# Chunk-selected attention and a gated MLP on one core: eight-tile bounds, half-row scores, transposes by DMA, and a written order

## The chip, the core and the metric

The kernel runs on one core of a Trainium2 chip. The core has five engines with instruction queues of their own: TensorE (PE; matrix products and transpositions), VectorE (DVE), ScalarE (ACT), GpSimd (POOL) and SyncE (SP, which here only issues DMA transfers). They meet through semaphores alone: an engine takes its instructions in the order written, and a wait holds up all that is queued behind it. The metric is device time in microseconds (us). Before the change it is 266.71 us, the median of three runs (265.65 to 267.24). The profiled execution spans 262.9 us from its first to its last instruction.

## The reference

Two parts, over 4 batches of 768 rows.

Attention: 8 heads of 64 columns per batch, 32 heads in all. The keys of a head form 24 chunks of 32 rows. For each chunk the minimum and maximum of every key column are taken, and each query gets an upper bound of its score on each chunk:

```
ub = sum(max(q * k_min, q * k_max))          # q, k_min, k_max: 64 columns
ub = where(chunk of q >= chunk, ub, -1e9)
top_chunks = argsort(ub)[-6:]                # six chunks per query
mask = (chunk of key in top_chunks) & (row of q >= row of key)
attn = softmax(where(mask, q k^T / 8, -1e9)); x = attn v
```

The MLP, on x of shape 4 x 768 x 512:

```
u, v = split(gelu(x w_in))                   # 512 + 512 columns
v_n  = layernorm(v) * g_ln
out  = x + (u * (w_sg v_n + b_sg)) w_out     # w_sg mixes the 768 rows
```

## The kernel before

**Pairs and quads.** Two heads make a pair p (16 of them), two pairs a quad g (8). `loads` (L525) brings q, k and v as f32, 192 KB for each head, three buffers of each, never more than four transfers in flight (`WINDOW`). `kside` transposes k on PE in two halves of 384 rows (L540), takes the chunk minima and maxima on DVE (L546, into `W`; L559 turns the maxima into differences) and copies k^T to bf16 on ACT: L551 for the first four pairs, in two copies of 64 partitions to `KA` and `KB`, and L555 for the others, in one copy of 128 partitions, with a DMA moving the second head from `KA` to `KB` (L563) and another putting the chunk indicator `IND` beside it (L565). `qside` does the same with q (L575, L580), makes `rT` = max(q, 0) on DVE (L584) and casts q to bf16 on POOL (L587, L589, L592).

**Bounds and selection.** Since max(q kmin, q kmax) = q kmin + max(q, 0)(kmax - kmin), `select` computes the bounds of a quad as f32 products on PE (L613): two PSUM banks of 288 query rows each, and in a bank four tiles of 64x32 side by side, one for each head. Only rows from 192 on need it; earlier rows have at most six chunks. DVE transposes the bounds in 32x32 blocks (L621), finds the sixth largest (L629: 18 top-eight instructions), compares (L632) and transposes the result back: straight into `QA` and `QB` for the first two quads (L640), else into `Dt` (L644), from which DMA copies take it (L649). A chunk not selected is marked 1 there, and `IND` holds -480 on that chunk's keys, so that the product of the extended q and k is the score with the mask in it.

**Heads.** `head` multiplies q and k in blocks on or below the diagonal into two PSUM tiles of 1024 columns (L677), ACT takes the exponential (L682), POOL clears what lies above the diagonal (L686), PE multiplies with v, which has a column of ones (L696, L703), and DVE divides (L711, L713) into `XS`. When a pair is done, `xtrans` transposes its columns of x on PE (L723) and DVE copies them to `xT` (L727). w_sg is transposed in the same way, once (L735, L739).

**MLP of a batch.** When four pairs are done: `moe_h` computes v (L751, gelu L755, statistics L758 and L760, 1/sqrt on POOL L764, normalizing L767) and u (L777, gelu L782); `moe_g` mixes the rows (L794, on two PSUM banks), scales and adds the bias on DVE (L801, `vsT`), multiplies by u on DVE (L805), and multiplies by w_out (L814); DVE adds x (L820), and SP stores (L823). It runs among the attention of later pairs; the last batch's MLP stands alone at the end.

**The order.** `schedule` is a list planner: with costs and priorities it decides, when the kernel is built, each engine's order, and it gives PSUM slots and semaphores accordingly. The small PSUM tiles (four banks, PSG) are split by purpose. `fill` puts dummy products (L463) where PE would wait at the start, so that its clock stays up.

Of the kernel before, what the change touches and what calls it, by code (L numbers as in the profile page):

```python
# [13 lines left out]
LAT = {"pe": 0.15, "act": 0.20, "dve": 0.12, "pool": 0.15, "sp": 0.05}  # L14
TABLE_SWITCH = 1.3
WINDOW = 4


class PsumTile:


    def __init__(self, cls, slots=None):
        self.cls = cls
        self.slots = slots
        self.left = 0
        self.slot = None
        self.end = 0.0
        self.ops = []
# [6 lines left out]
class PsumClass:  # L35
    def __init__(self, aps):
        self.aps = aps
        self.owner = [None] * len(aps)

    def tile(self, slots=None):  # L40
        return PsumTile(self, slots)


class Op:
    __slots__ = ("eng", "fn", "cost", "prio", "deps", "dma", "ps", "alloc", "table", "burst",
                 "start", "end", "pos", "waits", "inc", "count", "idx", "lane", "bulk", "port")


class Program:
# [3 lines left out]

    def __init__(self):
        self.ops = []
        self.writer = {}
        self.readers = {}
        self.dma_sems = {}
        self.base = 0.0

    def op(self, eng, fn, cost, reads=(), writes=(), ps=(), alloc=None, dma=None, table=None,
           burst=None, prio=None, lane=0, bulk=False, port=False):
        o = Op()
        o.bulk = bulk
        o.port = port or (eng == "pool" and dma is None)
        o.lane = lane
        o.idx = len(self.ops)
        o.eng, o.fn, o.cost, o.dma, o.table, o.burst = eng, fn, cost, dma, table, burst
        o.prio = (self.base if prio is None else prio) + 1e-4 * o.idx
        deps = {}  # L70
        ps = tuple(ps) + ((alloc,) if alloc is not None else ())
        o.ps, o.alloc = ps, alloc
        for t in ps:
            t.left += 1
            for x in reversed(t.ops):
                if x.eng != eng:
                    deps.setdefault(x.idx, False)
                    break
            t.ops.append(o)
        for r in reads:  # L80
            w = self.writer.get(r)
            if w is not None:
                deps[w] = True
        for r in writes:
            w = self.writer.get(r)
            if w is not None:
                deps[w] = True
            for x in self.readers.get(r, ()):
                deps.setdefault(x, False)
        for r in reads:  # L90
            self.readers.setdefault(r, []).append(o.idx)
        for r in writes:
            self.writer[r] = o.idx
            self.readers[r] = []
        if dma is not None:
            last = self.dma_sems.setdefault(dma, [])
            if last:
                deps[last[-1]] = True
            last.append(o.idx)
        o.deps = deps  # L100
        self.ops.append(o)
        return o

    def schedule(self):
        ops = self.ops
        succ = [[] for _ in ops]
        ndep = [len(o.deps) for o in ops]
        alloc = {o.alloc: o for o in ops if o.alloc is not None}
        for o in ops:
            hold = set()  # L110
            for t in o.ps:
                a = alloc[t]
                if a is not o:
                    hold.update((d, a.idx) for d in o.deps if d < a.idx and d not in a.deps)
            for d, a in hold:
                if a not in succ[d]:
                    succ[d].append(a)
                    ndep[a] += 1
            for d in o.deps:
                succ[d].append(o.idx)  # L120
        ready = {e: [] for e in ENGINES}
        rt = [0.0] * len(ops)
        for o in ops:
            if ndep[o.idx] == 0:
                ready[o.eng].append(o.idx)
        free = {e: 0.0 for e in ENGINES}
        order = {e: [] for e in ENGINES}
        table = None
        burst_left = {}
        for o in ops:  # L130
            if o.burst is not None:
                burst_left[o.burst] = burst_left.get(o.burst, 0) + 1
        cur_burst = None
        pool_owner = {}

        def slot_for(t, now):
            best = None
            for i, own in enumerate(t.cls.owner):
                if t.slots is not None and i not in t.slots:
                    continue  # L140
                at = 0.0 if own is None else (own.end if own.left == 0 else None)
                if at is not None and (best is None or at < best[0]):
                    best = (at, i)
            return best

        n = 0
        dma_free = 0.0
        soft_free = 0.0
        flight = []
        held = {"pool": 0.0, "dve": 0.0}  # L150
        while n < len(ops):
            pick = None
            for e in ENGINES:
                cands = []
                for i in ready[e]:
                    o = ops[i]
                    t = max(rt[i], free[e])
                    if o.alloc is not None and o.alloc.slot is None:
                        s = slot_for(o.alloc, t)
                        if s is None:  # L160
                            continue
                        t = max(t, s[0] + 0.15)
                    if e == "act" and o.table is not None:
                        if cur_burst is not None and o.burst != cur_burst:
                            continue
                        if o.table != table:
                            t += 0.0
                    if o.port:
                        t = max(t, held["pool" if e == "dve" else "dve"])
                    if o.bulk and len(flight) >= WINDOW:  # L170
                        t = max(t, ops[flight[-WINDOW]].end)
                    cands.append((t, o.prio, i))
                if not cands:
                    continue
                tmin = min(c[0] for c in cands)
                best = min((c for c in cands if c[0] <= tmin + 0.02), key=lambda c: c[1])
                if pick is None or best[0] < pick[0]:
                    pick = (best[0], e, best[2])
            if pick is None:
                raise RuntimeError("no operation can be scheduled")  # L180
            t, e, i = pick
            o = ops[i]
            ready[e].remove(i)
            if o.alloc is not None and o.alloc.slot is None:
                at, s = slot_for(o.alloc, t)
                old = o.alloc.cls.owner[s]
                if old is not None:
                    for x in old.users:
                        o.deps.setdefault(x, False)
                o.alloc.slot = s  # L190
                o.alloc.cls.owner[s] = o.alloc
                o.alloc.users = []
            cost = o.cost
            if e == "act" and o.table is not None:
                if o.table != table:
                    cost += TABLE_SWITCH
                    table = o.table
                if o.burst is not None:
                    cur_burst = o.burst
                    burst_left[o.burst] -= 1  # L200
                    if burst_left[o.burst] == 0:
                        cur_burst = None
            o.start = t
            if o.port:
                held[e] = t + cost
            if o.bulk:
                if len(flight) >= WINDOW:
                    o.deps[flight[-WINDOW]] = True
                flight.append(i)
            if o.dma is not None:  # L210
                if e == "pool":
                    soft_free = max(soft_free, t + 1.0) + 2.0 * cost
                    dma_free = max(dma_free, t + 0.3) + 0.4 * cost
                else:
                    dma_free = max(dma_free, t + 0.3) + cost
                free[e] = max(t + 0.6, dma_free - 3.0) if e == "sp" else t + 0.9
                o.end = (soft_free if e == "pool" else dma_free) + 2.0
            else:
                free[e] = t + cost
                o.end = t + cost  # L220
            for p in o.ps:
                p.left -= 1
# [144 lines left out]
def act(n):  # L367
    return 0.19 + n / 1200.0
# [540 lines left out]
```

The softmax here doesn't subtract the row's maximum and nothing guards it: scores larger than these inputs give would overflow.

## Time and profile before

| | us |
|---|---|
| time, median of three | 266.71 |
| span of the profile | 262.9 |
| PE busy | 225.0 (86%) |
| DVE busy | 197.7 (75%) |
| ACT busy | 153.4 (58%) |
| POOL busy | 76.9 (29%) |
| PE's share of the chain of work that ended last | 50% |
| DVE's share of that chain | 32% |

PE is pipelined, and its busy time holds the latency of each product too, so 86% is not 86% of its peak. The chain is followed back from the last instruction, at each step to what released it. Transfers: 32.39 MB in all, a mean of 123 GB/s, but most of it in the first third. Groups of instructions are named by their line, with the tiles they write and read, the count, the mean time of one and the idle time ahead.

### The profile page before, as it was taken

The page shows a single profiled execution, that of the slowest core. Times are in us where ns is not written, and L with a number is a line of the kernel's source. Part 1 is how long each engine was busy: PE and PEld are TensorE (multiplying, and loading weights), DVE is VectorE, ACT ScalarE, POOL GpSimd, SP SyncE. Part 2 cuts the span into 40 slices and gives each one's busy share as a digit, 9 for nine tenths or more (in the row PEclk, how much of TensorE's full clock was granted, in tenths as well). Part 3 has the DMA queues.
Part 4 walks back from the last instruction along what each step waited for, and adds up shares of the span by engine and source line. Part 5 has one row for each costly group of instructions (what it writes and reads, how often), then busy time and mean ns, then how long its engine had stood idle before and what let it go on. Part 6 is the DMA issues. An engine that isn't in the chain of part 4 may idle for free.

```text
span 262.9 us, 5801 instructions
## 1 busy us (share of the span) xinstructions
PE 225.0 (86%) x2242; PEld 140.2 (53%) x2258; DVE 197.7 (75%) x561; ACT 153.4 (58%) x232; POOL 76.9 (29%) x99
## 2 busy tenths in 40 slices
PE   8886488987996599998899899997998998689874
PEld 3444256665743378655555577566445765434431
DVE  6949579787558668989677988886588876467883
ACT  1444848977649545655784974658757645846000
POOL 3353728653201424222212433134210211202000
PEclk9999689999999569999999999999999999999999
DMA  7999999998999904856751443122101031100033
GB/s 167 201 225 202 205 221 197 235 227 175 199 209 160 212 19 109 228 132 182 163 122 43 100 100 135 51 95 55 38 6 24 2 122 58 64 0 0 0 123 120
DMA packets 84652, 32.39 MB, mean 123 GB/s; under 512 B 77232, under 2 KB 80912, under 8 KB 84624
## 3 DMA queue, kind: packets, MB, share of 16 engines
q1 hardware_dynamic: 82608, 29.26, 48.1%
q0 software_dynamic: 2016, 2.75, 6.4%
q8 instruction: 18, 0.29, 0.5%
q14 instruction: 10, 0.08, 0.1%
HBM read 24.77 MB, written 6.29 MB: 118 GB/s over the span
## 4 chain that ended last, share of the span: by engine, by line
PE 50%; DVE 32%; ACT 9%; issue 6%; POOL 1%; POOLq 1%
PE PSG L794 9%; PE PSG L814 8%; PE PSC L677 8%; PE PSG L613 7%; DVE W L546 5%; ACT E L682 5%; DVE vhat L767 5%; PE PSG L751 4%; PE PSG L696 4%; DVE vsT L801 3%; PE PSG L777 3%; DVE uT L805 3%; DVE m_1 L629 2%; DVE XS L713 2%; PE PSC L463 2%
## 5 line engine op out<-in xcount | busy, mean ns | idle before, releaser
L682 ACT ACTIVATE E<-PSC 128x1024 bf16<-128x1024 f32 (+1 forms) x96 | 84.5, 920 | 44.7 <-PE PSC L677 44.1
L686 POOL TENSOR_SCALAR_AFFINE_SELECT E<-E 128x768 bf16<-128x768 bf16 x32 | 28.5, 892 | 59.9 <-ACT E L682 59.6
L794 PE MATMUL PSG<-wsgT,vhat 128*128 128x384 bf16 x192 | 36.6, 335 | 4.9 <-DVE vhat L767 3.0
L546 DVE TENSOR_REDUCE W<-PSG 128x12 f32<-128x384 f32 x64 | 33.1, 543 | 7.5 <-PE PSG L540 7.3
L677 PE MATMUL PSC<-QB,KB 128*128 128x128 bf16 (+1 forms) x224 | 26.0, 253 | 2.7 <-ACT E L682 2.7
L677 PE MATMUL PSC<-QA,KA 88*128 88x128 bf16 (+1 forms) x224 | 24.8, 249 | 3.4 <-ACT E L682 2.6
L794 PEld LDWEIGHTS PSG<-wsgT,vhat 128*128 128x128 bf16 x192 | 18.3, 100 | 17.6 <-DVE vhat L767 3.0
L801 DVE SCALAR_TENSOR_TENSOR vsT<-PSG,glnT,bsgbc 128x384 f32<-128x384 f32 x32 | 19.7, 614 | 7.6 <-PE PSG L794 7.5
L814 PE MATMUL PSG<-woutb,uT 128*128 128x512 bf16 x88 | 21.8, 380 | 3.9 <-DVE uT L805 3.3
L777 PE MATMUL PSG<-xT,winb 128*128 128x384 bf16 x128 | 23.8, 327 | 0.4 <-DVE xT L727 0.3
L696 PE MATMUL PSG<-vx,E 128*128 128x65 bf16 x480 | 20.4, 195 | 4.1 <-ACT E L682 2.7
L696 PEld LDWEIGHTS PSG<-vx,E 128*128 128x128 bf16 x480 | 18.0, 99 | 10.0 <-ACT E L682 5.6
L751 PE MATMUL PSG<-winb,xT 128*128 128x512 bf16 x90 | 21.6, 379 | 1.3 <-DVE xT L727 0.9
L575 PE MATMUL PSG<-identF,qn 128*128 128x128 f32 x96 | 16.1, 283 | 6.7 <-ACT KB L551 3.6
L755 ACT ACTIVATE vgb<-PSG 128x512 f32<-128x512 f32 x24 | 14.1, 598 | 13.1 <-PE PSG L751 13.1
L820 DVE TENSOR_TENSOR osb<-PSG,XS 128x512 f32<-128x512 f32 x24 | 16.6, 691 | 6.4 <-PE PSG L814 5.9
L677 PEld LDWEIGHTS PSC<-QA,KA 88*128 88x128 bf16 x224 | 16.3, 99 | 9.5 <-ACT E L682 4.6
L580 ACT ACTIVATE qT<-PSG 128x384 f32<-128x384 f32 x32 | 15.5, 496 | 9.5 <-PE PSG L575 9.4
L782 ACT ACTIVATE uT<-PSG 128x384 bf16<-128x384 f32 x32 | 15.6, 490 | 9.1 <-PE PSG L777 8.8
L598 POOL CAST vx<-vn 128x768 bf16<-128x768 f32 x16 | 13.2, 830 | 24.1 <-PE PSG L703 19.2
L677 PEld LDWEIGHTS PSC<-QB,KB 128*128 128x128 bf16 x224 | 15.9, 100 | 7.8 <-ACT E L682 4.9
L758 DVE BATCH_NORM_STATS2 stats<-vgb 128x6 f32<-128x512 f32 x24 | 16.0, 681 | 4.7 <-ACT vgb L755 4.7
(69 smaller groups left out, 343.7 us busy)
## 6 DMA issues: line engine op xcount, KB each, us to landing
kn<-in_k_dram SPq DMA_DIRECT2D x32, 192.0 KB, 3.6
qn<-in_q_dram SPq DMA_DIRECT2D x32, 192.0 KB, 3.6
vn<-in_v_dram SPq DMA_DIRECT2D x32, 192.0 KB, 3.5
out_dram<-osb SPq DMA_DIRECT2D x24, 256.0 KB, 2.0
vgb<-in_moe_w_sg_dram POOLq DMA_DIRECT2D x6, 192.0 KB, 5.9
QB<-QA SPq DMA_DIRECT2D x12, 96.0 KB, 2.2
KB<-KA SPq DMA_DIRECT2D x12, 96.0 KB, 3.0
winb<-in_moe_w_in_dram POOLq DMA_DIRECT2D x4, 256.0 KB, 5.9
```

Of the source, the lines that this page charges most:

```text
L546: P.op("dve", lambda d, t=t, m=m, op=op, hf=hf: d.tensor_reduce(W[w][:, m, 12 * hf:12 * hf + 12], t.ap()[:, 0:TG].rearrange("p (c x) -> p ...
L613: r = e.matmul(t.ap()[32 * j:32 * j + 32, 0:n], W[w][lo:lo + 64, m, :], rhs, start=(m == 0), stop=(m == 1), tile_position=(lo, 32 * j))
L677: r = e.matmul(t.ap()[:, o:o + n], kt_[rows, 128 * kb:128 * kb + 128], qt_[rows, q0:q0 + n], start=True, stop=True, skip_group_check=True)
L682: P.op("act", lambda e, t=t, c0=c0, c1=c1: e.activation(E[es][:, c0:c1], t.ap()[:, 0:c1 - c0], ACTF.Exp, scale=SCALE), act(c1 - c0), reads ...
L686: P.op("pool", lambda g: g.affine_select(ev, ev, pattern=[[0, NT], [1, 128]], compare_op=ALU.is_ge, fill=0.0, base=0, channel_multiplier=- ...
L696: r = e.matmul(t.ap()[:, 65 * qb:65 * qb + 65], E[es][:, a:a + 128], vx[w][:, kb, i, :], start=first, stop=False, skip_group_check=True)
L751: r = e.matmul(t.ap()[:, 0:F], xT[s][:, dk, 128 * qt:128 * qt + 128], winb[:, dk, F:DFF], start=(dk == 0), stop=(dk == NDK - 1))
L777: r = e.matmul(t.ap()[:, 0:TG], winb[:, dk, 128 * fb:128 * fb + 128], xT[s][:, dk, TG * tg:TG * tg + TG], start=(dk == 0), stop=(dk == NDK ...
L794: r = e.matmul(t.ap()[:, 0:TG], vhat[s][:, sb, 128 * fb:128 * fb + 128], wsgT[:, sb, TG * tg:TG * tg + TG], start=(sb == 0), stop=(sb == N ...
L801: P.op("dve", lambda d, t=t, fb=fb, tg=tg, vs=vs: d.scalar_tensor_tensor(vsT[vs][:], t.ap()[:, 0:TG], glnT[:, fb:fb + 1], bsgbc[:, TG * tg ...
L814: r = e.matmul(t.ap()[:, 0:DM], gT[s][:, fb, 128 * qt:128 * qt + 128], woutb[:, fb, :], start=(fb == 0), stop=(fb == NF - 1))
L820: P.op("dve", lambda d, t=t, qt=qt, os_=os_: d.tensor_tensor(osb[os_][:], t.ap()[:, 0:DM], XS[:, (b % 2) * NT + qt, :], op=ALU.add), dve(D ...
```

## The change

The planner is gone: the order of all 1347 operations stands in the kernel as a table of names (`ORDER`), with the PSUM slot of each tile (`:2`) and, for operations that two engines can do, the engine (`@act`, `@dve`). `FILL` names the few places of dummy products. What is computed stays the same. The parts:

1. **Bounds in eight tiles.** A head's rows are cut in parts (two of 288 for most pairs), and the two heads of a pair stand on the two row halves of the array, so that eight 64x32 tiles of two banks are at work together. A part looks at fewer rows than before but needs small memsets (`uc`) where the causal limit cuts it. It serves PE time and gives DVE smaller pieces.
2. **The first two pairs are selected alone**, each in four parts of 192 rows, so that scores can start when one pair is there.
3. **The first four pairs are scored in row halves.** Both heads' k^T stay in one tile of 128 partitions (`KP`), as does q (`QP`); head 0 uses the upper 64 rows of the array, head 1 the lower. The mask comes in as a product of its own with 32 rows (`IND` times `Dt`) added in PSUM. So nothing needs to be copied into `QA`/`QB` there.
4. **For the other pairs** k^T is copied by ACT in two copies of 64 partitions (no `KB` and `IND` transfers), and q by POOL in two.
5. **x^T and w_sg^T by transposing DMA** on SP, but for the last pair's x^T, which stays on PE and is copied by DVE and ACT in halves. `XS` is laid out for it.
6. **POOL gates.** 17 of 32 products with u (`gm`) go to POOL, 15 stay on DVE; a third `vsT`.
7. **max(q, 0)** is made by ACT for 13 of the 16 pairs; 1/sqrt is done in two halves, so that normalizing can start on the first three tiles. Any small PSUM bank may be used for anything.

The core of the diff:

```diff
-            for hf in range(2):
-                t = ps_g.tile(t_slots(2 * g))
+            banks = [ps_g.tile(), ps_g.tile()]
...
+                for m in range(2):
+                    for j in range(len(tiles[0])):
+                        for i in range(2):
+                            cg, p, q0 = tiles[i][j]
+                            w, lo = p % 4, 64 * i
...
+                            r = e.matmul(banks[i].ap()[32 * cg:32 * cg + 32, 0:nq], W[w][lo:lo + 64, m, :], rhs,
+                                         start=(m == 0), stop=(m == 1), tile_position=(lo, 32 * cg))
...
+                                e.matmul(t.ap()[:, 512 * i + o + a - q0:512 * i + o + n],
+                                         IND[32 * cg:32 * cg + 32, 128 * kb:128 * kb + 128],
+                                         dt_[32 * cg:32 * cg + 32, a - d0:z - d0], start=fresh[i], stop=False,
+                                         skip_group_check=True, tile_position=(32 * cg, 0))
...
+                            r = e.matmul(t.ap()[:, 512 * i + o:512 * i + o + n],
+                                         KP[p][64 * i:64 * i + 64, 128 * kb:128 * kb + 128],
+                                         QP[p][64 * i:64 * i + 64, q0:q0 + n], start=fresh[i], stop=True,
+                                         skip_group_check=True, tile_position=(64 * i, 0))
...
+                P.op(f"xt{b}.{dk}", "sp", lambda e: e.dma_start_transpose(
+                    out=xT[s][:, dk, :].rearrange("p (j q) -> p j q", q=128),
+                    in_=XS[:, s, dk].rearrange("p j d -> p (j d)")), reads=rd, writes=[("xT", s, dk, hf) for hf in range(2)],
...
+            P.op(f"wsgT{j}", "sp", lambda e, j=j: e.dma_start_transpose(
+                out=wsgT[:, :, 128 * j:128 * j + 128], in_=wsgf[:, j, :]),
...
-        P.schedule()
...
+        P.arrange(ORDER)
```

The table around the first MLP, the last x^T, and the end (names: k and q loads lk, lq; transpositions kt, qt; bounds ub; scores s, exponentials e, values pv and pd; x by DVE xr, xs; xt transposes x; hv, hu, pt, ou the MLP's four products, gv, gu their gelus, vs, gm, oa what follows, os the store):

```
kt7.0:2 xr7 qt7.0:3 kn7.0 kt7.1:1 qe7.0 kw5 kx7.0 qb7 xs7 ... ub4:30 xt0.3 ... qt8.1:3 ... hu0.00:1 ud4.0 hv0.3:3
...
xt2.3 qt14.0:2 qe15.0 qr13 ou1.4:3 ... ub12:12 oa1.4 ... hv2.1:3
...
pt3.02:3 gu3.00 pt3.00:1 pt3.03:0 vs3.00 gm3.00@dve pt3.01:2 vs3.02 pt3.11:1 gm3.02@dve vs3.03 pt3.13:3 vs3.01 gm3.03
```

## The prediction

> **What bounds the kernel now.** I read the busy time by stretch first, cut where the work changes: until the first scores (23 us), until the first MLP matmul (64.4), until the last exponential (228.6), and the end. Columns: stretch, length, then busy us (and instructions) of PE, PE weight loads, DVE, ACT and POOL, TensorE clock, DMA share, GB/s.
>
> ```profile
> 0.00:23.00 23.00, 18.38 (x112) 9.47 (x114) 17.09 (x62) 8.09 (x16) 8.25 (x19) 1.00 0.90 193
> 23.00:64.40 41.40, 31.97 (x426) 22.06 (x427) 32.96 (x104) 30.32 (x48) 24.75 (x34) 0.92 1.09 211
> 64.40:228.60 164.20, 148.82 (x1552) 96.79 (x1564) 125.39 (x353) 106.25 (x156) 42.55 (x45) 0.97 0.46 107
> 228.60:262.90 34.30, 25.81 (x153) 11.87 (x155) 22.24 (x44) 8.76 (x15) 1.32 (x1) 1.00 0.12 47
> ```
>
> Three kinds of stage. Until 64.4 the DMA engines are full (share 0.90, then 1.09), and DVE holds the chain of waits. From 64.4 on PE is busy 91% of the time. At the end DVE paces PE. The DMA view of the first 64 us says what fills it (queues: packets, MB, share of 16 engines; issues: count, KB, us to landing):
>
> ```profile
> q1 hardware_dynamic: 38056, 10.25, 75.3%
> q0 software_dynamic: 2016, 2.75, 26.3%
> ...
> kn<-in_k_dram SPq DMA_DIRECT2D x17, 192.0 KB, 4.4
> qn<-in_q_dram SPq DMA_DIRECT2D x16, 192.0 KB, 4.3
> vn<-in_v_dram SPq DMA_DIRECT2D x16, 192.0 KB, 3.5
> ```
>
> So 49 loads of q, k and v and all weights pass in 64 us. SyncE's part runs at 10.25 MB / (0.753 x 64 us) = 0.213 MB/us; the weights of POOL's queue cost 0.263 x 64 / 2.75 = 6.1 us per MB. The timeline shows the start's chain: bounds, top-six, and four transposes of the mask on DVE ahead of the first scores.
>
> ```profile
> 16.47 0.69 PE L613 MATMUL PSG<-qT,W 64*32 64x288 f32 x8 [0.31 <-DVE rT L584]
> ...
> 19.20 1.47 DVE L629 MAX8 m_0<-U 128x8 f32<-128x8 f32 x18
> ...
> 22.28 0.77 DVE L640 STREAM_TRANSPOSE QA<-Dn 32x576 bf16<-32x576 bf16 x1
> ...
> 23.10 0.78 PEld L677 LDWEIGHTS PSC<-QA,KA 88*128 88x128 bf16 x11 [1.00 <-DVE QA L640]
> ```
>
> And the chain of waits near the end: the product vsT x uT alternates with vsT's own instruction on DVE, while PE waits.
>
> ```profile
> 244.20 0.63 DVE vsT L801
> 244.85 0.56 DVE uT L805
> 245.41 0.54 DVE vsT L801
> 245.98 0.56 DVE uT L805
> ```
>
> **What the Trainium skill says.** TensorE: Matmul & The Clock Gate, Back-to-back issue gap: matmuls follow each other after N/2.4 + 2.5 ns. The trace agrees: four 512-column matmuls of L751 come every 0.86 us, 4 x 0.216. So I count PE by columns, not by "busy" time, which holds the pipeline's latency. TensorEngine Tiling (Array Packing), Key Properties: changing the tiling mode drains the array. No drain stands out around L613 here, but the new score tiles change mode inside each tile. SBUF — State Buffer, SBUF: two separate sides: DVE in a two-port mode and POOL exclude each other for a whole instruction. The trace agrees: L584 took 0.99 us at 11.11, under a POOL cast, and 0.46 at 15.96. ScalarE: Activation LUTs, Table sets: relu is in every set, so putting max(q,0) on ACT should load no table; no row here shows it.
>
> **The change part by part.**
>
> PE per unit, by issue distance: K or Q transposition of three blocks 0.33 us; bounds 1.05 per bank, two banks per two pairs; scores of a head 2688/2.4 ns + 22 pieces x 2.5 ns = 1.18; its values 0.63 (21 x 30 ns); an xT or w_sg^T transposition 0.34; MLP of a batch 6 x 0.86 (hv) + 8 x 0.65 (hu) + 8 x 0.97 (L794) + 6 x 0.86 (L814) = 23.3.
>
> *Bounds in eight tiles.* Now a bank runs four products side by side, and the second bank follows. With eight tiles both banks' products run at once: at best one bank's 1.05 us per two pairs, at worst (no overlap of the row halves) still 2.10. I take 1.05, since four side by side gain nearly four now (8 products, each two records of 402 ns, in 1.10 us). From pair 6 on that saves 5 x 1.05 = 5.3 us on PE, the bounding engine. DVE pays for it: 18 transpositions and comparisons of half size instead of 8, and 26 small memsets (0.06 to 0.13 each, nearest row L624), some 3 us after 64.4, hidden beside PE.
>
> *x^T and w_sg^T by DMA.* Off PE: 12 x 0.34 + 6 x 0.34 = 6.1 us. Off DVE: L727 and L739, 8.9 + 3.2 us, less 0.5 for the last one, which stays on PE. New: 21 transposing transfers of 0.197 MB. The trace has none. The low price is Advanced Engine Details and Errata, X-Bar Transpose (TRN2): 350 GB/s or more, 0.56 us; the high one is the rate of this trace's SyncE queue, 0.92 us. I take 0.75, by the 261 GB/s of DMA: Bandwidth & Descriptors, Latency and other measured facts. A new wait: each xT sits in SyncE's queue behind xs, with loads and stores behind it, and hv of that batch waits for it. With a landing of 2.2 to 3.6 us (rows of section 6) against 2.2 us of PE work which the order puts between xt2.3 and hv2.1 (qt14.0 0.33, ou1.4 0.86, ub12 1.05), I take 1 us per batch, inside the unused time below, at worst 5.
>
> *First four pairs in halves, two selected alone.* The mask enters through small matmuls of 32 rows, so the four L640 transpositions (3.1 us per two pairs) and the QA/QB set-up memsets leave DVE. PE: 2688 columns for two heads at once (1.12 us) plus 2432 masked columns (1.01): 2.13 against 2.36 per pair, but with a mode change per tile perhaps 3.9. It does not matter while DMA sets the pace. First scores need one pair instead of two: at some 16 us instead of 23.
>
> *But the DMA floor stays.* In the new order, PE meets before its first hv: k of pairs 0 to 7, q of 0 to 8, v of 0 to 3, 42 loads, 8.26 MB; with bsg (0.39) and mask rows (0.15) 8.8 / 0.213 = 41 us. w_in and w_sg: 2.23 x 6.1 = 13.6. Ten transposes: 7.5. Together 62 us, and up to 1.09 of a share has been had, so 57 to 63. The first MLP starts at **60** against 64.4. By then the same is done on PE as before (31 transposition groups then, 34 now; both eight heads).
>
> *64.4 to 228.6.* PE work before: 3 MLPs 69.8, 33 transpositions 10.9, ten bounds 10.5, 24 heads x 1.81 = 43.4, xT and w_sg^T 6.1: 140.7, so 23.5 us not used. Of these 5 are the reduced clock at 80 to 100 us. After: 69.8 + 30 x 0.33 + 5 x 1.05 + 43.4 = 128.4. DVE falls: 125.4 - 6.1 (xT) - 3.2 - 4.4 (rT to ACT) - 12 x 0.575 (half of L805 to POOL) + 3 = 108. ACT rises, since K is now copied as two halves of 64 partitions (0.48 each, L551) in place of one of 128 and a DMA: 61 (24 x 2.54 for exps) + 32 x 0.48 + 15 x 0.44 + 7 x 0.7 (relu, by the 576/384 of L580's 0.49) + 22.6 (gelu) + 7.7 (tables) = 118. POOL rises to some 60. PE still leads. DVE free earlier shortens its waits (L767's 4.41 us at 85.7 before L794 starts), ACT at 80% lengthens others: unused time 19, at 15 to 29. **147 us.**
>
> *The end.* From the last exponential to hv 3.1, hv and hu 10.8, as now. From L794 on it took 16.8 us to the last osb. With four banks, three vsT and half the products on POOL, 8 x 0.97 + 6 x 0.86 + 0.4 + 0.7 = 14.1. With 3.1 for the last store: **31** against 34.3.
>
> Sum 60 + 147 + 31 = 238; the time is 3.8 above the span (266.7 against 262.9): 241.
>
> **The rivals.**
> 1. *ACT and the fixed order give it back.* Three engines at 73 to 87% wait for each other, 29 us unused in the middle: 64 + 157 + 32 = 253, time 257. For it: ACT gets 12 us more work there; against: it now waits 44 us for L677's scores, which is slack.
> 2. *Transposing transfers are slow or block SyncE's queue.* 5 us per batch, loads late behind them, first MLP at 68: 68 + 167 + 33 = 268, time **272, slower**. For it: the DMA is full to 64 us. Against: over the whole stretch from 64 us on its share is 0.46.
> 3. *The floor is softer and PE is fed.* First MLP at 54, 10 unused: 54 + 138 + 30 = 222, time 226. For it: a share of 1.17 at 50 to 60 us; against: the sum of bytes.
>
> **How the numbers follow.** Forecast 0.63, rival 1 0.17, rival 2 0.07, rival 3 0.13. The range 229 to 257 leaves out rival 2 and most of 3, and takes in the first MLP at 57 to 63, the transposes at both prices and 15 to 29 unused. Rival 2 alone is slower; of rival 1 a little falls within 0.5%: faster 0.91, same 0.02, slower 0.07.
>
> **What would show it.** First exponential near 16 us, but first MLP matmul no earlier than 57, DMA share near 1 until then. No DVE rows for xT but one. L613's successor near 1.0 us for all eight tiles. ACT near 170 us in all, DVE near 168, PE still the largest share of the chain of waits. The last product group paced by PE at 0.97. The prediction is wrong if xT's landing is above 6 us with PE waiting on it, if ACT ends most PE waits after 60 us, or if the clock drops in the less filled start.

## The result, and the profile after

| | before | after |
|---|---|---|
| time, median (lowest to highest), us | 266.18 (264.85 to 267.24) | 240.44 (238.46 to 243.46) |
| ratio of the two, 95% interval | | 0.9012 (0.894 to 0.9083) |
| span of the profiled execution | 262.9 | 237.4 |
| first exponential at | 23.8 | 17.7 |
| first MLP product at | 64.4 | 66.0 |
| last exponential ends at | 228.6 | 204.3 |

Here and below the ratios leave out runs that the chip slowed, while the medians and ranges hold all runs. The kernel is faster by 26 us, and the forecast was 241. But the sum came out right by luck, through errors that cancel: of the span, the prediction had 60 + 147 + 31 us for the three stages, the profile has 66.0 + 138.3 + 33.1 (a second one, of the same kernel, 69.2 + 138.7 + 33.2). So the experiments had to find out three things: why the start gained nothing, why the middle gained so much, and what the listed parts have to do with it.

The busy time by stage (same columns as before: stretch, length, busy us of PE, weight loads, DVE, ACT, POOL, then clock, DMA share, GB/s), cut at the same events:

```profile
0.00:66.00 66.00, 53.91 (x730) 32.70 (x738) 40.74 (x167) 43.32 (x74) 32.90 (x59) 1.00 1.14 191
66.00:204.30 138.30, 130.23 (x1437) 86.54 (x1449) 113.00 (x333) 115.33 (x175) 68.07 (x82) 1.00 0.61 130
204.30:237.40 33.10, 27.20 (x164) 13.96 (x164) 21.34 (x45) 8.65 (x17) 6.16 (x7) 0.97 0.27 94
```

In the middle, PE is now busy 94% of the time (91% before), and the granted clock is 1.00 where it was 0.97. DVE's work there fell by 12 us, that of ACT and POOL rose by 9 and 26. The start still has a DMA share above 1.

The DMA view of the first 64 us (queues: packets, MB, share of 16 engines; issues: count, KB, us to landing):

```profile
q1 hardware_dynamic: 38926, 9.97, 95.2%
q0 software_dynamic: 1296, 2.03, 17.9%
...
wsgT<-vgb SPq DMA_TRANSPOSE x4, 5.8
xT<-XS SPq DMA_TRANSPOSE x4, 6.5
```

SyncE's queue moved a little less than before (9.97 against 10.25 MB) but held the engines for 95.2% instead of 75.3%. The loads are the 42 (16 of k, 18 of q, 8 of v) that the prediction counted. New are the transposing transfers, which land after some 6 us. The chain of waits at the end of the start, and beside it the last division of x on DVE and SyncE's own timeline:

```profile
60.58 5.39 DMA xT<-XS
65.97 0.05 issue
66.02 0.82 PE PSG L889 x4
```

```profile
54.61 3.21 SPq L824 DMA_TRANSPOSE xT<-XS  x1
...
60.00 0.55 DVE L815 TENSOR_TENSOR XS<-PSG,rden 128x384 bf16<-128x384 f32 x1
60.58 1.21 SPq L824 DMA_TRANSPOSE xT<-XS  x1
61.83 5.29 SPq L496 DMA_TRANSPOSE wsgT<-vgb  x3
```

The first MLP product (L889) waits for the last x^T of batch 0. Between the two transfers of x^T SyncE stands idle, from 57.82 to 60.58 us: x itself is only ready at 60.55. So what ends the start here is the late x and then the 5.39 us until its transfer has landed. The five transposing transfers take 9.6 us of SyncE's time, and the next loads of k stand behind them until 67.2. At the end of the middle the chain reads:

```profile
204.67 0.69 DVE osb L939
...
206.69 2.92 DMA out_dram<-osb
209.64 0.70 DVE osb L939
210.39 2.76 PE PSG L854 x12
213.16 3.26 PE PSG L889 x20
```

PE has a sum ready for DVE to write (L939), but all three `osb` tiles are still waiting to be stored: the stores stand in SyncE's queue behind a transposing transfer that is issued only at 204.01. PE's products of the last batch (L854) then wait for DVE to empty a bank, though for no more than 0.22 us. In the last group PE sets the pace, with 0.98 us for six L909 (6.84 for 42), as forecast:

```profile
217.38 1.95 PE PSG L889 x12
219.33 6.84 PE PSG L909 x42
226.26 0.63 DVE vsT L916
```

### The profile page after: what moved, and what is told of

It reads as the page before. It is cut to its first block, busy times and chain, and to the rows that moved or that the text cites. A ratio compares the mean times of both kernels' runs of the same rounds, so it can differ in the third digit from the quotient of the medians.

```text
span 237.4 us, 6067 instructions
## 1 busy us (share of the span) xinstructions
PE 211.3 (89%) x2329; PEld 133.2 (56%) x2351; DVE 175.1 (74%) x543; ACT 167.3 (70%) x264; POOL 107.1 (45%) x147
## 4 chain that ended last, share of the span: by engine, by line
PE 65%; DVE 14%; ACT 12%; DMA 4%; issue 2%; POOL 0%; POOLq 0%; SPq 0%; DVEq 0%; ACTq 0%
PE PSG L909 11%; PE PSC L775 9%; PE PSG L889 9%; PE PSG L854 8%; PE PSG L932 5%; PE PSG L796 5%; DVE W L535 4%; PE PSG L528 3%; ACT E L745 3%; PE PSG L623 3%; PE PSG L984 3%; PE PSG L561 3%; ACT E L779 2%; DMA xT<-XS 2%; ACT qT L567 2%
## 5 line engine op out<-in xcount | busy, mean ns | idle before, releaser
L779 ACT ACTIVATE E<-PSC 128x1024 bf16<-128x1024 f32 (+1 forms) x72 | 62.8, 916 | 11.3 <-PE PSC L775 10.9
L681 POOL TENSOR_SCALAR_AFFINE_SELECT E<-E 128x768 bf16<-128x768 bf16 (+3 forms) x40 | 29.3, 745 | 27.1 <-ACT E L779 19.3
L909 PE MATMUL PSG<-wsgT,vhat 128*128 128x384 bf16 x192 | 35.2, 326 | 1.5 <-DVE XS L815 1.4
L745 ACT ACTIVATE E<-PSC 128x1024 bf16<-128x1024 f32 (+3 forms) x26 | 21.7, 858 | 7.5 <-PE PSC L735 7.2
L909 PEld LDWEIGHTS PSG<-wsgT,vhat 128*128 128x128 bf16 x192 | 17.9, 98 | 12.7 <-DVE XS L815 1.6
L854 PE MATMUL PSG<-winb,xT 128*128 128x512 bf16 x93 | 21.9, 379 | 1.4 <-ACT qT L567 0.9
L922 POOL TENSOR_TENSOR uT<-vsT,uT 128x384 bf16<-128x384 f32 x17 | 16.0, 947 | 14.9 <-DVE vsT L916 14.8
L889 PE MATMUL PSG<-xT,winb 128*128 128x384 bf16 x128 | 22.3, 326 | 0.4 <-DMA xT<-XS 0.3
L932 PE MATMUL PSG<-woutb,uT 128*128 128x512 bf16 x86 | 21.7, 379 | 0.9 <-POOL uT L922 0.3
L874 POOL TENSOR_TENSOR rstd<-rstd,neghalf 128x3 f32<-128x3 f32 x8 | 7.6, 948 | 32.9 <-DVE rstd L870 32.9
L775 PE MATMUL PSC<-QA,KA 96*128 96x128 bf16 (+2 forms) x168 | 19.3, 246 | 1.7 <-ACT qT L567 0.9
L939 DVE TENSOR_TENSOR osb<-PSG,XS 128x512 f32<-128x512 f32 x24 | 16.2, 686 | 5.7 <-DMA out_dram<-osb 4.4
L796 PEld LDWEIGHTS PSG<-vx,E 128*128 128x128 bf16 x480 | 17.7, 98 | 4.0 <-DVE osb L939 1.8
L813 DVE RECIPROCAL rden<-PSG 128x6 f32<-128x6 f32 x32 | 6.0, 189 | 18.3 <-PE PSG L804 18.2
L775 PE MATMUL PSC<-QB,KB 128*128 128x128 bf16 (+2 forms) x168 | 19.3, 246 | 0.1
L984 PE MATMUL PSG<-warm 128*128 128x512 bf16 x45 | 14.0, 430 | 5.3 <-ACT qT L567 1.6
```

What stands on the lines that cost most here:

```text
L681: P.op(f"af{h}.{r}", "pool", lambda g, ev=ev, cnt=cnt: g.affine_select(ev, ev, pattern=[[0, cnt], [1, 128]], compare_op=ALU.is_ge, fill=0. ...
L745: P.op(f"e{p}.{c}", "act", lambda e, t=t, o0=o0, nn=nn: e.activation(E[:, slot:slot + 2, o0:o0 + nn], t.ap().rearrange("p (i x) -> p i x", ...
L775: r = e.matmul(t.ap()[:, o:o + n], kt_[rows, 128 * kb:128 * kb + 128], qt_[rows, q0:q0 + n], start=True, stop=True, skip_group_check=True)
L779: P.op(f"e{h}h.{c}", "act", lambda e, t=t, c0=c0, c1=c1: e.activation(E[:, es, c0:c1], t.ap()[:, 0:c1 - c0], ACTF.Exp, scale=SCALE), write ...
L796: r = e.matmul(t.ap()[:, 65 * qb:65 * qb + 65], E[:, es, a:a + 128], vx[w][:, kb, i, :], start=first, stop=False, skip_group_check=True)
L854: r = e.matmul(t.ap()[:, 0:F], xT[s][:, dk, 128 * qt:128 * qt + 128], winb[:, dk, F:DFF], start=(dk == 0), stop=(dk == NDK - 1))
```

## The experiments

Each experiment starts from the changed kernel, timed beside the kernel before on the same chip; the changed kernel was run once more among them. In the profiles of the changed kernel (two runs) and of the kernels whose operations and order are the same until then, the first MLP product came between 65.4 and 69.2 us, so a shift of 3 us there is not evidence.

| run | median us | ratio to before (95%) |
|---|---|---|
| changed, again | 242.8 | 0.9081 (0.9037 to 0.9125) |
| w_sg^T on PE | 247.3 | 0.9259 (0.9223 to 0.9295) |
| and x^T of batch 0 | 254.4 | 0.9528 (0.949 to 0.9567) |
| all 21 on PE | 269.0 | 1.0088 (1.0055 to 1.0121) |
| one x^T on PE | 244.8 | 0.9124 (0.9078 to 0.917) |
| row halves in turn | 241.2 | 0.9007 (0.8969 to 0.9046) |
| order by a list rule | 263.8 | 0.9753 (0.9685 to 0.982) |
| list rule, all 21 on PE | 265.4 | 0.9887 (0.9829 to 0.9945) |
| stores early | 239.8 | 0.8987 (0.8937 to 0.9037) |
| few dummies | 241.0 | 0.9059 (0.9011 to 0.9107) |
| products on DVE | 241.6 | 0.906 (0.9021 to 0.9099) |

### The transposes, put back on PE step by step

My first theory (A) was that the transposing transfers overload the DMA and SyncE's queue ahead of the first MLP, so that putting them back on PE would gain time.

```diff
-            P.op(f"wsgT{j}", "sp", lambda e, j=j: e.dma_start_transpose(...
+            tw = ps_g.tile()
+            P.op(f"wsgT{j}", "pe", trw, ...)        # six 128x128 blocks
+            P.op(f"wsgE{j}", "dve", ...tensor_copy...)
...
-    XPE = ((B - 1, NDK - 1),)
+    XPE = ((B - 1, NDK - 1),) + tuple((b, dk) for b in (0,) for dk in range(NDK))
```

In the table of order each transposition takes the place of its transfer (w_sg's a few names later), or the next place where a bank is free. The changed kernel again:

> The changed kernel as it is, on the chip of the next three runs, so that they can be set against it: 240.4 us again, within 2. Every theory says the same.

w_sg^T (six):

> w_sg^T is transposed on PE (six blocks of six) and copied by DVE as before the change; x^T stays with the DMA. Theory A (transposing transfers overload the DMA engines and SyncE's queue ahead of the first MLP): six transfers fewer, first MLP matmul at 60 to 62 instead of 66, time 235 to 238. Rival B (the transfers are free, as the prediction took them, and the start is set by DVE and ACT): first MLP matmul stays at 65 to 67, PE has 2 us more, time 241 to 243.

These and the x^T of batch 0 (ten in all):

> w_sg^T and the four x^T of batch 0 on PE; the other eleven x^T by DMA. Theory A: no transposing transfer is left ahead of the first MLP, whose first matmul comes at 55 to 58, time 230 to 235. Rival B: first MLP matmul stays at 65 to 67, PE has 3.4 us more, time 242 to 244.

All 21:

> All 16 x^T and w_sg^T on PE, so part 5 of the change is undone in its order. Theory A: the start of the run before (first MLP matmul at 55 to 58), but PE gets 3.7 us more in the later stretch, where it has nothing to spare; stores at the end are no longer behind transposes in SyncE's queue, 1 to 2 us less: 232 to 237. Rival B: no gain at the start and 7 us more PE: 246 to 248.

Measured: the changed kernel again took 242.8, just outside the expected range. The three others took 4.5, 11.6 and 26.3 us more than it; with all 21, that is 1.25 us for each. Theory A fell: with ten transposes on PE the DMA was half empty from 50 us on, and the first MLP product came not earlier but at 78.5 us. The rival fell too, since its 2, 3.4 and 7 us are too few. With all 21, PE's busy time grew by 12.3 us (227.0 against 214.7), less than half of the loss. PE's waits in that kernel (what waited, for what, us in total, times, longest):

```profile
PE PSG L571 <- ACT xT L849: 2.9, 3, 1.0
PE PSG L806 <- ACT xT L849: 2.7, 3, 1.0
PE PSG L942 <- ACT xT L849: 2.6, 4, 0.8
```

The copies out of PSUM (L849) stand in ACT's fixed order, and whatever comes next in that bank waits for them: transpositions of q (L571), values (L806), products with w_out (L942). And in the stretch from 50 to 60 us of the kernel with ten on PE

```profile
50.00:60.00 10.00, 9.35 (x106) 5.65 (x105) 2.02 (x5) 6.75 (x12) 3.41 (x6) 0.54 0.43 61
```

the DMA share is 0.43 (theory A's overload is gone) and the clock is granted at 0.54, which costs up to 4.6 of the 9 us by which that start is longer. So this series can't tell what the transfers are worth. Nor does it show by itself that the order is to blame; that is tried further below.

### One transfer taken off the chain

```diff
-    XPE = ((B - 1, NDK - 1),)
+    XPE = ((B - 1, NDK - 1), (0, NDK - 1))
```

> Of the 21 transposing transfers one goes back to PE: the x^T of the last pair of batch 0, behind which the first MLP product waited 5.2 us for the transfer. If that transfer is what ends the start: its landing falls away for 0.5 us of PE and 0.5 us of copies, the first MLP product at 65 to 66 instead of 69 (same run series), time 238 to 240. If each operation put back into PE's queue costs over 1 us as in the three runs that put 6, 10 and 21 of them back: 243 to 245.

No gain. The chain of waits shows why:

```profile
64.51 0.52 PE PSG L832 x6
65.06 0.37 DVE xT L837
65.45 0.50 ACT xT L838
66.00 0.61 PE PSG L983 x2
67.51 0.50 ACT qT L566
...
69.20 0.65 PE PSG L888 x4
```

x^T was there at 66.0 us, 1.5 us after PE began on it. But the first MLP product (L888 here) stands in PE's queue behind transpositions of q, whose copy on ACT (L566) was now behind the copy of x^T, and behind dummies (L983). The transposition itself had been put behind the bounds (L622) in PE's order and waited for their bank; x had been ready at 62.6. So the transfer was not alone in ending the start; another chain of about the same length stood beside it. In the profiles of the runs "stores early" and "products on DVE", where all transfers are in place, the chain before the first MLP product also runs through bounds and transpositions of q, and no x^T is in it.

### What a transposing transfer costs

A kernel of transfers alone, in groups, each waiting for the one before:

```
8 loads of q | 8 plain copies | 8 transposing | 1 transposing | 8 x (load, transposing) | 24 stores
```

> Computes nothing of the reference (the output is zeros): SyncE alone issues, each group after the one before has landed, eight loads of q (192 KB), eight plain copies of 128x768 bf16 within the chip's memory, eight transposing transfers of the same tile, one alone, eight loads alternating with eight transposing transfers, and the stores. If the transposing transfer is what loads the start (theory A's remaining half): a group of eight takes more than 1.5 us per transfer against about 0.9 us per load, SyncE's issue of one takes over 1 us, and the mixed group takes about the sum of the two. If the price of the prediction holds (rival): 0.75 us each, eight in about 6 us plus one landing, and issue near the 0.6 us of a load.

The DMA view of 4 us within the transposing group, and SyncE's timeline, first group and mixed group:

```profile
q1 hardware_dynamic: 2404, 0.59, 77.1%
```

```profile
1.82 5.37 SPq L25 DMA_DIRECT2D ld<-in_q_dram  x8
...
36.58 1.28 SPq L28 DMA_TRANSPOSE tr<-xs  x1
37.91 0.58 SPq L25 DMA_DIRECT2D ld<-in_q_dram  x1
38.53 1.25 SPq L28 DMA_TRANSPOSE tr<-xs  x1
```

Three transfers (0.59 MB) held the engines for 0.771 x 4.0 us: 1.03 us each, 0.191 MB/us, about as long as a load of the same size (the eight loads took 8.8 us with the engines full: 1.1 each). The price in the prediction, 0.75, was too low, its high end, 0.92, nearly right. The eight plain copies of the same tile held the engines for 0.66 of 6.64 us, 0.55 us each: transposing takes nearly twice that. What sets the transfers apart from loads is SyncE: 1.25 us to issue one, against 0.58. In the mixed group a pair came every 1.92 us, little more than the sum of the two issues, at a DMA share of 0.90: no further loss from mixing. So neither expectation is quite met: above the prediction's price, below the 1.5 us that theory A named.

### The order of all operations, made anew by a rule

```diff
-ORDER = """
-W02 zB3 lk0.0 W00 warm0 J0 ...
+ORDER = """   # same names and engines, sorted by the rule; banks by the rule too
```

> The same operations on the same engines, but the order and the banks come from a simple list rule (each time the engine's ready operation with the earliest start, then priority), not from the table in the changed kernel. If the gain is in the operations (the prediction's reasoning, by sums of work): 243 to 250 us. If it is in the fitted order (rival): 257 us or more, most of the 26 us gone, with PE's busy work unchanged and its unused time up by 15 us or more.

The rival is right. With every part of the change in it, this kernel is at 0.9753, against 0.9012 and 0.9081. By stages (columns as above; the profile is of a run of 263.25 us, while the ratio rests on two of the six, of 258.93 and 262.17 us, so these stages hold some 1 to 4 us more):

```profile
0.00:73.10 73.10, 56.86 (x713) 32.62 (x721) 37.31 (x145) 42.00 (x69) 40.89 (x71) 0.88 1.16 195
73.10:228.00 154.90, 140.25 (x1466) 92.10 (x1476) 114.99 (x359) 117.16 (x179) 60.61 (x70) 0.97 0.54 115
228.00:261.40 33.40, 25.15 (x154) 13.34 (x156) 19.46 (x41) 9.13 (x17) 5.59 (x6) 0.97 0.13 48
```

DVE, ACT and POOL do the same work in the middle to within 2, 2 and 8 us, but the stage takes 154.9 us against 138.3: the 128.4 us that the prediction counted for PE, and 26.5 unused. Some 4 of these are the clock (0.97 of 140 us), the rest is waiting. The rule is a simple one of mine, not the planner of before, so the 18 to 20 us between the two orders (0.067 to 0.074 of 266) are what this rule leaves, not what any planner must leave; and the dummies are bound to operations, so that they too stand less well. The clock was lower over the whole kernel, 0.95 in these two runs against 0.98 to 1.00 in the changed kernel, and how much of the 18 to 20 us is the clock was not separated. The operations of the kernel before were not put under this rule, so the run does not show what the new operations are worth in an equal order.

### The transposes once more, under that rule

> All 21 transposing transfers back on PE, as in the run at 269.0 us, but here the order of all operations is made anew by the list rule of the run at 263.8 us, which had them by transfer. PE gets 12.3 us more busy work (the 269.0 run's 227.0 against 214.7), of which about 7 is issue, DVE 9.4 us, ACT 6.6 us. If the transfers themselves are worth PE's time (the prediction's step): 268 to 275 us, a ratio of 1.00 to 1.03 against the kernel before. If the 26 us in the fixed order came from the order no longer fitting its operations: 262 to 266 us, a ratio of 0.975 to 0.995.

The order is made by the same rule in both: 0.9887 against 0.9753, 1.3%, or 3.6 us for 21 transposes, about 0.17 us each. The two intervals nearly touch, so by them anything from 1 to 6 us is possible. That is neither the 26 us of the fixed order nor nothing; the 6 to 7 us of PE issue that went off PE lie at or above the upper end. The expectation of 262 to 266 us is met. But these orders leave PE unused for some 26 us of the middle, which can hide added work; what the transfers are worth in an order fitted to either set was not tried. By stages:

```profile
0.00:66.60 66.60, 56.50 (x747) 33.69 (x747) 40.79 (x152) 42.90 (x73) 41.99 (x72) 0.97 1.10 208
66.60:226.00 159.40, 143.33 (x1574) 94.24 (x1574) 120.35 (x372) 122.96 (x191) 60.83 (x70) 1.00 0.37 89
226.00:260.90 34.90, 27.29 (x156) 13.76 (x156) 19.76 (x41) 9.35 (x17) 5.61 (x6) 0.93 0.12 46
```

Without transposing transfers the start is 6.5 us shorter, the middle 4.5 and the end 1.5 us longer. In sum the two profiled runs are equal, because the one with transfers is the run of 263.25 us; so the split into stages does not explain the 3.6 us. What was left of theory A may have a foothold here, if the transfers cost time in the start. The clock speaks against taking them for the whole of the 6.5 us (0.97 here, 0.88 there).

### Bounds, one row half after the other

```diff
-                for m in range(2):
-                    for j in range(len(tiles[0])):
-                        for i in range(2):
+                for i in range(2):
+                    for m in range(2):
+                        for j in range(len(tiles[0])):
```

> The bounds with the loop over the two row halves outermost, so that the second bank's products come after the first's instead of between them; same products, same order of everything else. If the overlap of the row halves is what gives 1.05 us per two pairs (the prediction's step): L623 takes near 2.1 us per two pairs, all eight units 8 us more of PE, five of them where PE leads: 245 to 248 us. Rival: two banks written in turn overlap just as well, because PE takes a product as soon as its tile is free: 241 to 243, as the changed kernel.

The rival is right: 0.9007. The timeline has the same unit in the changed kernel, then in this one (start, us):

```profile
87.46 0.72 PE L623 MATMUL PSG<-qT,W 64*32 64x288 f32 x16
87.97 0.69 PE L623 MATMUL PSG<-rT,W 64*32 64x288 f32 x16
```

```profile
87.83 0.74 PE L623 MATMUL PSG<-qT,W 64*32 64x288 f32 x16
88.33 0.72 PE L623 MATMUL PSG<-rT,W 64*32 64x288 f32 x16
```

32 records of 0.40 us pass in 1.20 and 1.22 us. Eight tiles side by side do give what the prediction took (1.05 by issue for two banks, where a bank had 1.10 before), but how the products alternate has no part in it.

### Stores ahead of transposing transfers

```diff
-... os2.0 xt3.0 ... os1.4 pd29 xt3.1 ... xt3.2 ... os2.3 xs30 os2.1 os2.2 ...
+... oa1.4 os1.4 ... oa2.0 os2.0 ... oa2.2 os2.2 ...     # each behind what it reads; xt3.* likewise
```

> Only SyncE's order changes: the stores of batches 1 and 2 stand right behind the sums they store, and the transposing transfers of batch 3 right behind their division; in the changed kernel a store of batch 1 stood in SyncE's queue until 201 us, and five stores of batch 2 behind two transposing transfers until 205. If that is why the end came out 2 us longer than forecast: DVE's waits of 4 to 5 us in all for the stores at 200 to 210 us go, the end from the last exponential takes 30.5 to 31.5 instead of 33.1 us, time 238 to 240.5. Rival: hv of the last batch is held by the order on PE or the last x^T anyway: 241 to 243, as the changed kernel.

0.8987, not to be told from the changed kernel, and its end took 33.5 us. DVE waits for stores 5.3 us instead of 4.4. SyncE's timeline says why:

```profile
197.62 2.46 SPq L823 DMA_TRANSPOSE xT<-XS  x1
200.12 3.45 SPq L943 DMA_DIRECT2D out_dram<-osb  x3
204.40 1.22 SPq L823 DMA_TRANSPOSE xT<-XS  x1
```

The stores again came just behind a transposing transfer of 2.46 us, only another one. DVE's longest wait for a store had been 1.7 us, before 208.7; now it was 3.3 us, before 202.5. With that, the 24 products of hv (L853) ran without a gap, in 5.34 us from 207.62 on, and the end was no shorter. So the stores do hold DVE up behind transposing transfers on one queue, but that this made the end longer than forecast is not shown; this run speaks against it.

### Fewer dummies, and all products with u on DVE

```diff
-    "s1.2": 2, "s2.5": 4, "s2.2": 1, "s3.0": 2, "qt7.1": 2, "pv6": 8, "ub4": 3, ... "hu3.11": 1, }
+    "s1.2": 2, }
```

> The dummy products from the scores of pair 2 on are left out (29 of 61), all else stays. If they cost time where the wait they were meant for is over (they stand in the chain of waits at 36 and at 57 to 80 us): 1 to 4 us less, 238 to 241, with the first MLP product earlier by as much. Rival, they keep the clock up: the granted clock from 50 to 70 us falls below 0.9, and the time stays or rises to 242 to 245.

The edit takes out 31 of 65 dummies, not 29 of 61 as the expectation counts. 0.9059: no change that the runs can tell. The rival's clock came true (0.59 from 50 to 70 us, where the two profiles of the changed kernel had 1.00 and 0.90 to 0.93), its longer time didn't: the first MLP product came at 67.8 us, within the spread named above. Neither did the gain.

```diff
-... gm0.03 ... gm0.01 ...
+... gm0.03@dve ... gm0.01@dve ...       # 17 names
```

> All 32 products with u on DVE, as in the kernel before; all else stays. If the split matters as the prediction has it (DVE paced the last group by 1.2 us per product pair, PE's 0.98 paces it now): the end 2 to 3 us longer, and in the middle DVE gets 17 x 0.6 to 0.86 = 10 to 15 us more in 138 us, at over 90% of its time, so 2 to 5 us more there: 246 to 250. Rival: DVE has room in the middle and the products on POOL slow it by their port anyway: only the end shows, 243 to 245.

0.906, and 241.6 us: below both expectations, and no change that the runs can tell. The rival is right that DVE has room in the middle, but the end did not cost what it expected. The last group's chain in this kernel:

```profile
223.29 0.54 DVE vsT L916
223.85 0.56 DVE uT L922
224.41 1.05 DVE vsT L916 x2
225.46 0.46 DVE uT L922
...
231.28 2.78 PE PSG L932 x12
```

DVE paces the group once more, as it did before the change. Yet from the group's first product to the first of L932 it took 11.2 us (220.09 to 231.28), against 10.7 (219.33 to 230.05) with the split. So the split is worth 0.5 us here. The rest of what the end gained came from elsewhere. In the chain of the kernel before, products with w_out (L814) stood between the two groups of L794, which had two banks; now they come last, and any bank may be used. Which of the two, banks or order, did it was not tried apart.

## Why the prediction held, and where it did not

**First scores.** Near 16 us forecast, 17.7 measured. Right in kind.

**"Ten transposes: 7.5."** This is the term of the start's sum that failed in its price. Alone the transfers take 1.03 us each, so 10.3 us, and the sum becomes 41 + 13.6 + 10.3 = 65. In place they seem to take more: of the 0.952 x 64 us for which SyncE's queue held the engines, its other 8.8 MB at the prediction's 0.213 MB/us would be 41, which leaves 2.4 us for each of the eight transposing transfers that were issued by then (an estimate). The Trainium skill, Advanced Engine Details and Errata, X-Bar Transpose (TRN2), says that transposing transfers are as fast as others and names 350 to 400 GB/s. The first holds beside loads in 256-byte rows (1.03 against 1.1 us) but not beside plain copies of the same tile (0.55); the figure does not hold, since 0.191 MB/us is 191 GB/s. The 261 GB/s that the prediction took its price from is not reached either.

**"The DMA floor", 60.** That 65 lies beside the 66.0 measured is not yet a cause. The prediction then allowed for a share of up to 1.09; 1.14 was had, and still 66 us passed. The trace shows SyncE idle from 57.82 to 60.58 us for want of x (the DMA share was 0.64 from 56 to 58 us, 1.21 from 58 to 60): what the chain shows at the end of the start is late x, and then the landing of its transfer, 5.39 us, where the prediction had taken 2.2 to 3.6. Late loads can still have made x late; in the second profile of the changed kernel the chain runs from a load of v that took 7.29 us to land. Under the list rule the start was 6.5 us shorter without the transfers; in the fixed order, one of them taken off the chain brought nothing. I count the price and the late x as shown, and what made x late as open.

**The middle, 147.** The work on PE was counted at 128.4 us and the eight-tile bounds came out as costed. (One of the 18 transposes counted as going off PE, the last pair's x^T, stands after this stretch: 0.3 us.) For the count by columns the prediction cites the Trainium skill, TensorE: Matmul & The Clock Gate, Back-to-back issue gap. There N/2.4 + 2.5 ns is the gap of an isolated matmul, and for a stream of 512 columns a shorter one is named, 131 ns; the 216 ns in this trace fit the formula, so the count stands on the trace. What was mis-sized is the unused time: 19 forecast at 15 to 29, 9.9 measured. About 5 us of that is the clock, which the count of before had named (0.97 of 149 us) and which I left in; it was granted in full now. The rest is waiting: PE's waits over the whole span, summed by releaser, fell from 18.0 to 7.2 us for DVE and little for ACT (12.1 to 10.8).

**What those 12.3 us of counted work are worth was not understood.** The prediction reasons as if work taken from PE shortened the stage by itself, and treats the fixed order only as a risk (rival 1). The runs say that the order counts for more: with the same operations in an order by a simple rule, the middle takes 154.9 us, 9 less than before the change, and the start 9 more. Of the 26 us, 18 to 20 are lost with the fitted order, some of that perhaps to the clock. Rival 1 feared that the fixed order gives the gain back; here most of the gain is lost without it, and all of it is lost where the order is left as it is and the operations change, as in the series with PE transposes. That the planner of before, or the rule, would have served the old operations worse or better than the new ones was not tried.

**The end, 31.** 33.1. The last group is as forecast: 0.98 us on PE, and 14.2 us from the first L909 to the end of the last sum, 14.1 forecast. Its reason, half the products on POOL, is worth only 0.5 us. Of the 2 us that are missing, 1.2 lie between the first product of hv (207.36) and the first L909 (219.33), 12.0 us where 10.8 were forecast, and 0.8 between the last sum and the end, 3.9 us where 3.1 were forecast. The prediction had named stores queued behind xs and x^T in SyncE's queue, and put the cost at the start of hv in the middle. Such stores did hold DVE up, from 207 us on, but in the run "stores early", where hv ran without a gap, the end was as long. What made it longer stays open.

**ACT and DVE.** ACT 170 forecast, 167.3 measured. DVE 168 forecast, 175.1: some 4 of the 7 us are products with u that were held up while POOL worked (below).

**The signs of being wrong.** Of the three that the prediction names, two came. In the first 64 us the x^T landed after 6.5 us (median), and PE waited for one of them. And from 60 us on, ACT ended most of PE's waits, 5.7 of 10.1 us; yet this came about because DVE's waits had nearly gone, and not because ACT's had grown. The clock did not drop: it was 1.00 in the start.

So errors of +6, -9 and +2 us made an error of about zero. The range of 229 to 257 holds what was seen, and rival 3's middle (10 unused, 138 us) was the right one.

## What to carry to other kernels

Where several engines are near 80 to 90% busy and each takes its work in a fixed order, the sum of saved work alone did not say here how much would be gained; the order decided much of it. When you put one operation in or take one out to test it, make the order anew by the same rule for both sides, or the test measures the misfit too. Look behind a wait before you remove it: here a second chain, or the same queue's next transfer, stood within a microsecond or two. And look at single instructions, not only at means or merged lines: the 860 ns below are a mean that hardly any instruction took, and a merged line of two transfers in 7.18 us held 2.76 us in which SyncE only waited.

## What the runs showed of the hardware

- A transposing transfer of 0.197 MB took 1.03 us of the 16 DMA engines and 1.25 us of SyncE alone, against 0.55 and 0.61 us for a plain copy of the same tile. In a crowded kernel SyncE needed up to 3.2 us for one, and it landed after 2.8 to 7.3 us.
- A DVE instruction with both inputs in SBUF can be held up by POOL for whole instructions. The longest product with u on DVE (L922) took 3.52 us, while POOL worked without a gap on a cast, two products and a copy:

```profile
86.77 3.52 DVE L922 TENSOR_TENSOR uT<-vsT,uT 128x384 bf16<-128x384 f32 x1
```

```profile
86.53 0.84 POOL L586 CAST vx<-vn 128x768 bf16<-128x768 f32 x1
87.31 1.79 POOL L922 TENSOR_TENSOR uT<-vsT,uT 128x384 bf16<-128x384 f32 x2
89.05 0.82 POOL L479 COPY KB<-IND 64x768 bf16<-64x768 bf16 x1
```

  The median of the 15 products on DVE was 558 ns, as in the kernel before (557 ns for 32); their mean was 860 ns, against 571 before and 692 with all 32 on DVE. Under the list rule with all transposes on PE, the same split gave a mean of 578: what is lost depends on which instructions meet. The instructions that write `XS` and `osb`, which have one input in PSUM, kept their 551 and 686 ns (550 and 683 with no product on POOL). The Trainium skill, SBUF — State Buffer, SBUF: two separate sides, has the shared ports exclusive, for a whole instruction, also for a DVE instruction with two inputs in SBUF while a POOL instruction reads; that agrees. In the changed kernel it ate nearly half of what moving products to POOL was to bring: 17 x 571 ns gone, 15 x 289 ns added.
- The granted clock fell to 0.54 over ten microseconds in a start with ten more transposes on PE, and to 0.59 over 20 us without the later dummies; in the two profiles of the changed kernel it was 1.00, and 0.90 to 0.93, there.
- max(q, 0) on ACT took 687 ns for 576 columns, without a table load of its own: there are eight table loads before the change and eight after.
